# Two chained mixtures of experts after a recurrent attention: the first mixture's second product in float32 for all of F instead of half of it

## The chip, the cores and the metric

The kernel runs on one core of one Trainium2 chip. The metric is the device time of one execution in microseconds (us); the kernel before takes 814.17 us, the median of three runs from 814.04 to 814.33.

## The reference, cut to what matters

```python
# x: (3072, 384), the output of the attention, token by token
def _moe_ref(x, w_gate, w1, w2):               # first mixture, E = 8, F = 1024
    order = np.argsort(-(x @ w_gate).flatten())    # greedy, each expert takes 3072 / 8 = 384 tokens
    ...
    for e in range(E):
        mask = assigned == e
        h = np.maximum(x[mask] @ w1[e], 0.0)       # first product, 384 -> 1024
        out[mask] = h @ w2[e]                      # second product, 1024 -> 384
def _moe2_ref(x, modality_id, w_gate, modality_bias, w1, w2):   # second mixture: the same products,
    ...                                            # each token goes to its best expert and is scaled
```

## The kernel before, in words

The program has three stages on one core. The attention fills the first 235 us or so. Then come the eight experts of the first mixture, one after the other (`job` for j = 0 to 7), until about 560 us, and behind them the second mixture in units of up to 256 tokens (j = 8 and up).

For one expert TensorE (PE) works on 384 gathered tokens. F is cut into eight blocks f of 128. The first product of a block (line 837) has nine matmuls of 384 columns: each float32 operand is split into a high part of type float32r (`w1h`, `xh`) and the remainder (`w1l`, `xl`), and three products high x high, high x low and low x high are added up over three blocks of the 384 inputs. ScalarE (ACT) writes relu of the result to `hh` (line 841).

The second product adds up over f into three PSUM tiles `po`, one for each 128 tokens t. It has two forms, chosen by the table WHOLE for each half of F (blocks 0 to 3 and 4 to 7). In a whole half, `hh` is plain float32, the weights go by DMA straight into the tile `w2h`, and each (f, t) is a single float32 matmul (line 710), which the profile shows as two records of LDWEIGHTS and MATMUL. In a split half the weights land in `wraw`, ACT casts them to a high part (line 753), VectorE (DVE) or, once in the program, GpSimd (POOL) subtracts to get the low part (line 757), DVE makes the remainder `hl` of the hidden values (line 845), and each (f, t) has three matmuls (lines 712, 713, 714). In the kernel before, the experts of the first mixture have their first half whole and their second half split. In the split case the names of the weight pieces both read `w2l` in the profile, since both parts lie in one tile of that name.

While one expert is computed, the same engines prepare the next: `search` finds the next expert's threshold (three passes: DVE compares in `g` line 997, PE counts on line 1010, DVE makes `ind` line 1011, PE sums on line 1024 and, at the end, 1049 from `bm`), `listing` makes the list of its tokens (lines 1096 to 1146) and gathers them to `xg`, and `score2` and `route2` score the finished tokens for the second mixture. All of this is written into the instruction streams by `tick`, a planner that advances coroutines between blocks; each engine then runs its stream strictly in that order and waits by semaphores. Second products are held back in `pend` and flushed in pairs of blocks (blocks 0 and 1, 2 and 3, 4 and 5), 6 and 7 one by one beside the next expert's first blocks.

Of the kernel before, what the change touches and what calls it, by code (L numbers as in the profile page):

```python
# [37 lines left out]
E = 8  # L38
# [393 lines left out]
HALF = (7, 11)  # L432
PICKS = {5: (0, 2, True), 6: (2, 3, True), 7: (3, NU, False)}
NLC = 40
WHOLE = {**{j: 1 for j in range(E)}, E: 2, E + 1: 2, E + 2: 1}
PAGE = 256
GROUPS = {1: 6, 3: 6, 4: 3, 5: 3, 6: 3, 7: 3}
GM = 6
# [147 lines left out]
class Moe:  # L586
# [108 lines left out]
    def w2half(self, j, c):  # L695

        W, n, s = self.W[j], WHOLE.get(j, 0), slice(1536 * c, 1536 * c + 1536)
        if c < n:
# [17 lines left out]
    def weights(self, j, idx, first, every):  # L716
# [4 lines left out]
        def fetch():  # L721
            for h in range(4):
                yield from self.wait(f"lo{j - 1}.{2 * h + 1}")
                if j == 0 and h > 0:
                    yield from self.wait("g0")
                whole = h % 2 and h // 2 < WHOLE.get(j, 0)
                if whole:
# [14 lines left out]
        def split():  # L742
            for q in range(8):
                if q // 2 % 2 and q // 4 < WHOLE.get(j, 0):
                    continue
                yield from self.wait(f"raw{j}.{q // 2}")
                if j == 0 and q == 1:
                    yield from self.wait("x0")
                new = ("w1h", "w1l") if q == 0 else ("w2h", "w2l") if q == 2 else ("w2hl",) if q == 6 and WHOLE.get(j) else ()
                for n in new:  # L750
# [54 lines left out]
    def job(self, j, nt, after):  # L805
# [10 lines left out]
        def second(f, hh, hl, ts=range(nt)):  # L816
            self.until(f"lo{j}.{2 + 4 * (f // 4) + f % 4 // 2}")
            if f == 0:
                st["po"] = [self.po.tile([128, 512], FT, name="po") for _ in range(nt)]
            for t in ts:  # L820
                s = slice(128 * t, 128 * t + 128)
                o = st["po"][t][:, 0:DM]
                self.second_terms(j, f, s, o, hh, hl)
                if f == FB - 1:
                    after(st["po"], t)
            if f == FB - 1 and t == nt - 1:
                del self.W[j]

        for f in range(FB):
# [5 lines left out]
            for k in range(KB):  # L835
                for a, b in ((w1h, xh), (w1h, xl), (w1l, xh)):
                    nc.tensor.matmul(ph, a[:, f // 4, k, s], b[:, k], start=(n == 0), stop=(n == 3 * KB - 1))  # L837
                    n += 1
            whole = f // 4 < WHOLE.get(j, 0)
            hh = self.hp.tile([128, 512], FT if whole else FR, name="hh", bufs=4)[:, 0:T]  # L840
# [8 lines left out]
            self.pend.append(lambda *a, f=f, hh=hh, hl=hl: second(f, hh, hl, *a))  # L849
            keep = PACE["fl"] + (WHOLE.get(j, 0) > 0 and f % 2 == 0 and f > 1)  # L850
            self.flush(keep if f or len(self.pend) < 5 else 3)
# [796 lines left out]
```

## Time and profile before

| quantity | value |
|---|---|
| median of three runs | 814.17 us |
| the profiled execution | 810.52 us |
| its span, first to last instruction | 808.8 us |
| PE busy over the span | 713.9 us, 88% |
| DVE busy over the span | 631.8 us, 78% |
| ACT busy over the span | 352.1 us, 44% |
| POOL busy over the span | 413.1 us, 51% |
| mean granted clock of PE | 0.953 |

The profiled execution is 3.65 us below the median, and its span 1.7 us below its own time. Busy times are unions of the records of an engine, and the records of matmuls that follow each other overlap, because matmuls are pipelined: how long a run of them holds PE is read from the start of the first to the start of what follows.

### The profile page before, as it was taken

To read this page: it belongs to the slowest core of one execution; us is meant where nothing else is said; L and a number is where in the kernel's file an instruction comes from. 1 tells how busy PE (TensorE), PEld (TensorE's weight loads), DVE (VectorE), ACT (ScalarE), POOL (GpSimd) and SP (SyncE) were. 2 spreads that over 40 slices of the span, in tenths; PEclk is the share of its full clock that TensorE was granted. 3 is DMA by queue.
4 is the path that set the end of the run, shared out by engine and by line. 5 is a ranking of instruction groups with operands and counts; after the bars stand their busy time and mean duration, and the time that the engine had idled before them with its cause. 6 is when DMAs were issued, how large, how long until landed. Compare 5 with 4: busy or idle time off the path is not lost.

```text
span 808.8 us, 13793 instructions
## 1 busy us (share of the span) xinstructions
PE 713.9 (88%) x4889; PEld 633.7 (78%) x4889; DVE 631.8 (78%) x1575; ACT 352.1 (44%) x756; POOL 413.1 (51%) x371
## 2 busy tenths in 40 slices
PE   6887778878787798999999999999999999999993
PEld 4776667777754577878787878878778999999993
DVE  7999999999978877687876866847776668677770
ACT  3454545545422224333332433323345556666650
POOL 5788876878715413121211212135558766776640
PEclk8898988889899999999999999999999999999998
DMA  8567767667305235251533424264438766776740
GB/s 284 137 177 174 192 163 183 172 173 193 89 31 186 88 99 173 74 183 50 170 104 112 143 74 157 59 206 138 152 126 288 243 224 218 254 255 219 237 161 24
DMA packets 35199, 129.08 MB, mean 160 GB/s; under 512 B 5225, under 2 KB 14580, under 8 KB 35120
## 3 DMA queue, kind: packets, MB, share of 16 engines
q0 software_dynamic: 17568, 83.82, 30.8%
q1 hardware_dynamic: 16832, 43.95, 20.0%
q8 instruction: 40, 0.66, 0.4%
q10 hardware_dynamic: 720, 0.34, 0.2%
q14 instruction: 39, 0.32, 0.1%
HBM read 113.88 MB, written 14.60 MB: 159 GB/s over the span
## 4 chain that ended last, share of the span: by engine, by line
PE 48%; DVE 30%; issue 10%; DMA 5%; POOL 3%; ACT 2%; POOLq 0%; SPq 0%; DVEq 0%; ACTq 0%
PE ph L837 18%; PE po L710 9%; DVE pf L110 5%; PE po L712 4%; PE po L714 4%; PE po L713 4%; DVE suf L104 3%; DMA ch<-in_ch 2%; DVE pe L116 2%; DMA wraw<-in_w1b,wi 2%; DVE pc L107 2%; PE px L1190 2%; DVE rp L112 2%; DVE g L997 2%; PE px L1010 1%
## 5 line engine op out<-in xcount | busy, mean ns | idle before, releaser
L841 ACT ACTIVATE hh<-ph 128x256 fp32r<-128x256 f32 (+3 forms) x160 | 68.4, 428 | 223.4 <-PE ph L837 204.4
L837 PE MATMUL ph<-xh,w1h 128*128 128x256 f32 (+1 forms) x480 | 154.4, 322 | 1.0 <-DVE hl L845 1.0
L837 PE MATMUL ph<-xl,w1h 128*128 128x256 f32 (+1 forms) x480 | 146.2, 305 | 0.5 <-DVE xl L785 0.2
L837 PE MATMUL ph<-xh,w1l 128*128 128x256 f32 (+1 forms) x480 | 146.3, 305 | 0.0
L139 PE MATMUL pa<-rbd,kh 128*128 128x256 f32 x192 | 64.8, 496 | 46.2 <-ACT rbd L125 46.2
L837 PEld LDWEIGHTS ph<-xh,w1h 128*128 128x128 f32 x480 | 90.6, 189 | 10.6 <-issue 5.0
L837 PEld LDWEIGHTS ph<-xl,w1h 128*128 128x128 f32 x480 | 90.8, 189 | 3.1 <-DVE xl L785 1.4
L710 PE MATMUL po<-w2h,hh 128*128 128x384 f32 x272 | 93.1, 489 | 0.0
L837 PEld LDWEIGHTS ph<-xh,w1l 128*128 128x128 f32 x480 | 90.8, 189 | 0.0
L845 DVE SCALAR_TENSOR_TENSOR hl<-ph,hh 128x256 fp32r<-128x256 f32 (+1 forms) x108 | 49.7, 461 | 51.2 <-ACT hh L841 46.7
L139 PEld LDWEIGHTS pa<-rbd,kh 128*128 128x128 f32 x192 | 45.3, 248 | 56.5 <-POOL ru L131 43.0
L713 PE MATMUL po<-w2l,hh 128*128 128x384 f32 x264 | 88.5, 335 | 0.0
L753 ACT CAST w1h<-wraw 128x768 fp32r<-128x768 f32 x88 | 73.2, 833 | 12.5 <-DMA wraw<-in_w1a,ix 8.8
L498 POOL DMA_INDIRECT wraw<-in_w1a,ix x16 | 16.5, 1034 | 121.3 <-issue 53.0
L710 PEld LDWEIGHTS po<-w2h,hh 128*128 128x128 f32 x272 | 49.5, 190 | 28.8
L757 DVE TENSOR_TENSOR w1l<-wraw,w1h 128x768 fp32r<-128x768 f32 x66 | 64.6, 979 | 7.6 <-ACT w1h L753 7.4
L498 POOL DMA_INDIRECT xg<-xd,ix x24 | 31.3, 1305 | 76.2 <-DVE ix L1146 61.1
L757 POOL TENSOR_TENSOR w1l<-wraw,w1h 128x768 fp32r<-128x768 f32 x22 | 41.2, 1876 | 49.5 <-ACT w1h L753 49.4
L169 ACT ACTIVATE cv<-tk,cb 128x56 f32<-128x56 f32 x192 | 47.2, 328 | 39.2 <-DVE cb L166 39.2
L757 DVE TENSOR_TENSOR w2l<-wraw,w2h 128x768 fp32r<-128x768 f32 x44 | 47.8, 1086 | 11.5 <-ACT w2h L753 11.5
L712 PE MATMUL po<-w2h,hh 128*128 128x384 f32 x160 | 55.2, 345 | 0.0
L714 PE MATMUL po<-w2h,hl 128*128 128x384 f32 x160 | 53.8, 337 | 0.1
(350 smaller groups left out, 1766.9 us busy)
## 6 DMA issues: line engine op xcount, KB each, us to landing
tk<-in_tk SPq DMA_DIRECT2D x24, 608.0 KB, 6.6
ch<-in_ch SPq DMA_DIRECT2D x42, 288.9 KB, 5.4
xd<-y SPq DMA_DIRECT2D x24, 193.0 KB, 2.7
x2d<-x SPq DMA_DIRECT2D x8, 579.0 KB, 4.1
ch<-in_ch SPq DMA_DIRECT2D x23, 192.0 KB, 5.8
ch<-in_ch SPq DMA_DIRECT2D x1, 962.5 KB, 8.8
ch<-in_ch SPq DMA_DIRECT2D x1, 770.5 KB, 8.9
ch<-in_ch SPq DMA_DIRECT2D x2, 256.0 KB, 5.1
```

Source lines behind the costliest of these rows:

```text
L139: nc.tensor.matmul(pa[:, 2 * a:2 * a + 2], t["kh"][:, a], t["rb"][:, a], start=True, stop=True)
L169: nc.scalar.mul(cv[:, h], t["v"][:, DE * h:DE * h + DE], cb[:, h:h + 1])
L498: nc.gpsimd.indirect_dma_start(out=out, out_offset=None, in_=src, in_offset=bass.IndirectOffsetOnAxis(ap=idx, axis=0), bounds_check=bound, ...
L710: mm(o, hh[:, s], w[0][:, hs], start=a, stop=z)
L712: mm(o, hh[:, s], w[0][:, hs], start=a, stop=False)
L713: mm(o, hh[:, s], w[1][:, hs], start=False, stop=False)
L714: mm(o, hl[:, s], w[0][:, hs], start=False, stop=z)
L753: nc.scalar.copy(hi, r)
L757: self.turn[j][q].tensor_tensor(lo, r, hi.bitcast(FT), OP.subtract)
L837: nc.tensor.matmul(ph, a[:, f // 4, k, s], b[:, k], start=(n == 0), stop=(n == 3 * KB - 1))
L841: nc.scalar.activation(hh, ph, AF.Relu)
L845: nc.vector.scalar_tensor_tensor(hl, ph, 0.0, hh.bitcast(FT), op0=OP.max, op1=OP.subtract)
```

## The change

One number of the table WHOLE, which says how many halves of F are whole for expert j.

```diff
@@ -432,7 +432,7 @@
 HALF = (7, 11)
 PICKS = {5: (0, 2, True), 6: (2, 3, True), 7: (3, NU, False)}
 NLC = 40
-WHOLE = {**{j: 1 for j in range(E)}, E: 2, E + 1: 2, E + 2: 1}
+WHOLE = {**{j: 2 for j in range(E)}, E: 2, E + 1: 2, E + 2: 1}
 PAGE = 256
 GROUPS = {1: 6, 3: 6, 4: 3, 5: 3, 6: 3, 7: 3}
```

The table is read in `weights` (whether a half is fetched straight to `w2h` and not split), in `w2half` and `second_terms` (which matmuls), and in `job` (the type of `hh`, whether `hl` is made, and `keep`, whose condition is that WHOLE is over zero and so gives the same numbers as before). On PE the place of every other instruction stays the same; where the three split matmuls of an (f, t) stood, one float32 matmul stands. So on PE, in the first expert's block 6 (the tiles `po` are the three token blocks), before:

```order
L1049 MATMUL px_3091<-bm_87,ones_415 128x16
L712 MATMUL po_2766<-w2l_2681,hh_2938 128x384
L713 MATMUL po_2766<-w2l_2681,hh_2938 128x384
L714 MATMUL po_2766<-w2l_2681,hl_2940 128x384
L712 MATMUL po_2767<-w2l_2681,hh_2938 128x384
L713 MATMUL po_2767<-w2l_2681,hh_2938 128x384
L714 MATMUL po_2767<-w2l_2681,hl_2940 128x384
L712 MATMUL po_2768<-w2l_2681,hh_2938 128x384
L713 MATMUL po_2768<-w2l_2681,hh_2938 128x384
L714 MATMUL po_2768<-w2l_2681,hl_2940 128x384
L837 MATMUL ph_3125<-xh_2942,w1h_2905 128x384
```

and now, at the same place on PE:

```order
L1049 MATMUL px_3064<-bm_87,ones_415 128x16
L710 MATMUL po_2760<-w2h_2503,hh_2927 128x384
L710 MATMUL po_2761<-w2h_2503,hh_2927 128x384
L710 MATMUL po_2762<-w2h_2503,hh_2927 128x384
L837 MATMUL ph_3092<-xh_2929,w1h_2894 128x384
```

Nine rows became three, and what stands ahead and behind is the same.

On DVE, in the third expert, between the routing for the second mixture (lines 1225, 1227) and the search's `ind`, before:

```order
L1225 TENSOR_REDUCE mxo<-eq_3832 128x6
L845 SCALAR_TENSOR_TENSOR hl<-ph,hh 128x384
L1201 TENSOR_REDUCE se<-ex 128x3
L1202 TENSOR_SCALAR se<-se 128x3
L1203 RECIPROCAL x_3643<-se 128x3
L1204 COPY x_3643<-xg 128x3
L1011 TENSOR_SCALAR ind<-px,rem 8x64
```

and now, at the same place on DVE:

```order
L1225 TENSOR_REDUCE mxo<-eq_3749 128x6
L1201 TENSOR_REDUCE se<-ex 128x3
L1202 TENSOR_SCALAR se<-se 128x3
L1203 RECIPROCAL x_3561<-se 128x3
L1204 COPY x_3561<-xg 128x3
L1011 TENSOR_SCALAR ind<-px,rem 8x64
```

Only `hl` is gone from ahead of `ind`; the subtractions of line 757 for `w2l` go from DVE in the same way.

On POOL, in the first expert, the gathers of weights and the one subtraction that POOL has for the second product, before:

```order
L498 DMA wraw<-in_w1a,ix 128x1536
L498 DMA wraw<-in_w2a,ix 128x1536
L757 TENSOR_TENSOR w1l<-wraw,w1h 128x3x256 x2
L757 TENSOR_TENSOR w2l<-wraw,w2l 128x768
L498 DMA wraw<-in_w1a,ix 128x1536
```

and now, at the same place on POOL:

```order
L498 DMA wraw<-in_w1a,ix 128x1536
L498 DMA w2h<-in_w2a,ix 128x1536
L757 TENSOR_TENSOR w1l<-wraw,w1h 128x3x256 x2
L498 DMA wraw<-in_w1a,ix 128x1536
```

The gather of the second half has the same size and place and another target, and the subtraction is gone.

## Rows read from the trace of the kernel before

**Rows 1.** Windows: stretch, length, busy us (instructions), PE clock, DMA share, GB/s.

```profile
348.36:386.00 37.64, 35.37 (x274) 30.49 (x274) 30.05 (x115) 12.95 (x25) 8.96 (x7) 1.00 0.30 98
...
560.00:600.00 40.00, 40.00 (x238) 31.75 (x239) 29.80 (x106) 15.14 (x32) 18.81 (x15) 1.00 0.53 184
```

**Rows 2.** Waits of PE, 255 to 560 us: waiter, releaser, us, times, longest.

```profile
PE px L1010 <- DVE g L997: 7.0, 5, 2.2
PE px L1024 <- DVE ind L1011: 5.8, 7, 1.2
...
PE px L1049 <- DVE bm L1039: 1.8, 4, 0.7
PE px L1242 <- DVE tb L1234: 1.8, 2, 1.3
...
PE px L1111 <- DVE ef L1102: 1.3, 1, 1.3
PE px L1326 <- DVE vv L1320: 0.5, 1, 0.5
PE ph L837 <- DVE hl L845: 0.3, 1, 0.3
```

**Rows 3.** Timeline of PE in one expert: start, us, line, shapes, idle before.

```profile
350.94 4.12 PE L710 MATMUL po<-w2h,hh 128*128 128x384 f32 x12
354.89 0.73 PE L1190 MATMUL px<-wg,xt 128*128 128x8 f32 x6
...
362.10 4.04 PE L710 MATMUL po<-w2h,hh 128*128 128x384 f32 x12
365.97 0.49 PE L778 MATMUL px<-ident,xg 128*128 128x128 f32 x3
...
371.55 0.42 PE L712 MATMUL po<-w2l,hh 128*128 128x384 f32 x1
...
374.76 0.33 PE L837 MATMUL ph<-xh,w1h 128*128 128x384 f32 x1
...
376.32 0.33 PE L712 MATMUL po<-w2l,hh 128*128 128x384 f32 x1
...
377.88 0.33 PE L837 MATMUL ph<-xh,w1h 128*128 128x384 f32 x1
```

**Rows 4.** Instructions on tile `po`: duration ns min/median/max, starts, forms.

```profile
L710 PE MATMUL po<-w2h,hh x272: 483/486/590, 272.1 to 610.7; 128*128 128x384 f32 x136
...
L713 PE MATMUL po<-w2l,hh x264: 331/334/346, 295.5 to 795.5; 128*128 128x384 f32 x132
```

**Rows 5.** Timeline of DVE and PE around 360 us.

```profile
358.69 0.55 DVE L845 SCALAR_TENSOR_TENSOR hl<-ph,hh 128x384 fp32r<-128x384 f32 x1
...
359.75 0.26 DVE L1011 TENSOR_SCALAR ind<-px,rem 8x64 bf16<-8x64 f32 x1
...
360.07 0.19 PE L1024 MATMUL px<-ind,ones 128*128 128x64 bf16 x1 [1.19 <-DVE ind L1011]
```

**Rows 6.** Timeline of POOL, DVE and PE in the first expert.

```profile
265.93 1.87 POOL L757 TENSOR_TENSOR w2l<-wraw,w2l 128x768 fp32r<-128x768 f32 x1 [0.63 <-ACT w2l L753]
...
266.37 1.46 DVE L1163 COPY md<-xg 128x3 f32<-128x3 f32 x1
...
300.80 0.15 DVE L1163 COPY md<-xg 128x3 f32<-128x3 f32 x1
...
269.01 0.94 DVE L757 TENSOR_TENSOR w2l<-wraw,w2l 128x768 fp32r<-128x768 f32 x1
...
268.86 0.17 PE L1049 MATMUL px<-bm,ones 128*128 128x16 bf16 x1 [0.66 <-DVE bm L1039]
...
272.02 0.16 PE L1111 MATMUL px<-inc,tri 128*128 128x1 bf16 x1 [1.30 <-DVE ef L1102]
```

**Rows 7.** Timeline of POOL: two gathers of one expert.

```profile
380.65 1.00 POOL L498 DMA_INDIRECT w2h<-in_w2a,ix  x1 [0.30 <-PE po L714]
...
395.05 1.59 POOL L498 DMA_INDIRECT xg<-xd,ix  x1 [9.42 <-DVE ix L1146]
```

## The prediction, made before the changed kernel ran

> **What bounds the kernel now.** I read the windows by stage first. In a steady expert of the first mixture PE is busy 35.37 of 37.64 us at a granted clock of 1.00 (the upper of its two levels, 2.4 GHz), DVE 30.05, ACT 12.95; in the second mixture PE is busy all 40.00 us of a window [rows 1]. So from the second expert on PE sets the pace, with some 2.3 us an expert (37.64 - 35.37) in which it waits. Next I read for whom: between 255 and 560 us the waits of PE that DVE ended add up to 7.0 + 5.8 + 1.8 + 1.8 + 1.3 + 0.5 + 0.3 = 18.5 us [rows 2], nearly all of them links of the search for the next expert, a chain that goes from PE to DVE and back. Two things thus count in this change: what it does to PE's own work, and how much of those 18.5 us hangs on the DVE, ACT and POOL work that it takes away. Last I read PE's timeline, from the start of a run of matmuls to the start of what follows it, since the records overlap.
>
> **PE's own work.** For each expert the second half has 4 blocks x 3 token blocks = 12 (f, t), 96 in the 8 experts. In a split half PE goes through blocks 4 and 5 (18 matmuls) from 371.55 to 374.76, in 3.21 us, and through block 6 (9 matmuls) from 376.32 to 377.88, in 1.56 us, 0.173 us a matmul and so 0.52 us an (f, t) [rows 3]. Block 7 has the same nine, so 1.56 again; the three runs make 3.21 + 2 x 1.56 = 6.33 us an expert. In a whole half a pair of blocks (6 float32 matmuls, 12 records) takes 350.94 to 354.89, 3.95 us, where it stands behind a small bf16 matmul, and 362.10 to 365.97, 3.87 us, where it does not [rows 3]: 0.645 us an (f, t), two records of 0.32. In the changed kernel the pair 4, 5 stands behind the bf16 matmul of line 1049, so 3.95; blocks 6 and 7 are half a pair each, together 3.87. That is 7.82 us. The float32 form thus costs PE 7.82 - 6.33 = 1.49 us more an expert, and 8 x 1.49 = 11.9 us in all. It all lies on the engine that sets the pace, so this is the main term, and it makes the kernel slower.
>
> The Trainium skill has a rule on this (FP8 and Floating Point Precision, TensorE Precision Notes): true FP32 makes four passes through the array, while FP32 at reduced precision is read and truncated. The trace agrees in its direction, 0.645 us against 0.52 [rows 3]; it does not agree in the size that counting passes would give, which is a rival below.
>
> **What goes from the other engines.** Each expert loses four `hl` on DVE, 0.55 us each [rows 5], two subtractions of `w2l`, 0.94 us on DVE [rows 6], one of the 16 on POOL, 1.87 us [rows 6], and two casts on ACT. PE gains only where such an instruction stands ahead of a link that PE waits for. I went through PE's waits one by one:
>
> - Experts 2 to 4, `ind` behind `hl`: DVE runs without a pause from the token scores to `ind` at 359.75, with `hl` at 358.69 in between, and PE waits 1.19 us for it [rows 5]. Without `hl` the `ind` comes one slot of about 0.5 us earlier (its 0.55 us overlap their neighbours a little). 3 x 0.5 = 1.5 us, with what the wait for `bm` may gain.
> - The first expert is bound by the search. POOL's subtraction runs 265.93 to 267.80, and during it a copy of three elements a partition, `md`, takes 1.46 us on DVE where the same copy later takes 0.15 [rows 6]. With the subtraction gone DVE is 1.3 us earlier at `bm`, and PE's wait of 0.66 us ahead of line 1049 goes; PE also starts that matmul some 0.15 us earlier because the queue ahead of it is empty: 0.8 us. Then DVE's own `w2l` subtraction at 269.01 stands between `bm` and the list, and PE waits 1.30 us for the list at 272.02 [rows 6]; I let 1.1 of it go. Two `hl` further on stand ahead of a `g` and an `ind`: 0.3 and 0.4. Together 2.6 us.
> - The last expert: the routing chain that ends in `vv` is held up by an `hl` that waits for ACT; the waits of 0.5 for `vv` and 0.3 for an `hl` go [rows 2]: 0.8 us.
> - Others stay. The long waits for `g` in the second expert and for `tb` in experts 6 and 7 (1.3 the longest) [rows 2] end chains in which no removed instruction stands.
>
> The sum of the relief is 1.5 + 2.6 + 0.8 = 4.9, with 0.3 for small ones 5.2 us. Its bounds are 0, if another link is late in place of each, and 18.5 us, all that DVE ended [rows 2]. I take 5.2, since each term has its own row or place, and most of the 18.5 is the round trip itself.
>
> **What moves.** The second half's weights now land in the whole tile `w2h`, two of which exist. The gather for expert j + 1 must wait until expert j - 1 has finished with all eight blocks, where four were enough. In POOL's queue that gather stands at 380.65, when PE is at the last products of block 7 of that very expert [rows 7]. With the longer float32 products it would start perhaps 2 us later. Behind it stand two more gathers and then the gather of tokens, ahead of which POOL is idle for 9.42 us [rows 7]; the weights of those gathers are wanted an expert later. So I cost it at nothing; without that cover it would be 2 us an expert. The number of bytes stays, and on ACT nothing that PE waits for stood behind the two casts but in the first expert, which is counted above.
>
> **The sum.** 11.9 - 5.2 = 6.7 us. Made against the profiled execution: 810.52 + 6.7 = 817.2. The median of the runs shown is 3.65 us above that execution, and I carry the difference along: 814.17 + 6.7 = 820.9 us. No term lies behind 560 us, where PE is full and its instructions are the same, so the delay reaches the end.
>
> **The rivals.**
>
> 1. The relief does not come: each wait that goes is taken over by the next link of the same chain, which is a round trip and not a queue. Then only PE's work counts, 814.17 + 11.9 = 826.1. For it speaks that DVE often stands idle for PE in the chain; against it that in rows 5 and 6 DVE works without a pause ahead of the link.
> 2. The relief is much greater, and the kernel gets faster. The mechanism is the search chain on DVE: with 4 us less DVE work an expert the chain runs ahead, and all PE's waits on it vanish. The end of this is 11.9 - 18.5 = -6.6, 807.6 us; it decides for faster from the point where more than 11.9 + 1.6 of the 18.5 us go. For it speaks DVE's load of 30.05 us in 37.64 [rows 1]; against it that `g`, the largest entry, is waited for where no removed instruction precedes it. I would put this case at about 811.
> 3. The duration of a record is its price. The float32 record takes 486 ns and the split one 334 [rows 4], so an (f, t) would take 2 x 486 = 972 ns against 3 x 334 = 1002, and 96 x 0.03 = 2.9 us would be won on PE, before any relief: 814.17 - 2.9 - 5.2 = 806.1. Against it stands rows 3, where the same records start 0.32 and 0.17 us apart. The Trainium skill has the reason to choose by the starts (Trainium Kernel Development and Optimization, Performance Expectations): matmul busy time is a bad metric because matmuls are pipelined.
> 4. A float32 matmul costs four times a split one, 4 x 0.173 = 0.69 us, and the rows of a float32 pair understate it, because the run behind it starts late. Then 96 x (0.69 - 0.52) = 16.3, less 5.2, gives 814.17 + 11.1 = 825.3. This is what the rule on four passes named above would make of the row of the split form. Against it stands the pair's own rows, 3.87 us for six [rows 3].
>
> **How the numbers follow.** Forecast 0.75, rival 1 0.10, rival 2 0.06, rival 3 0.03, rival 4 0.06. Around the forecast the relief can be some 3 us more or less, 817.5 to 824. The range takes in most of rivals 1 and 4 above and a part of rival 2 below: 816 to 825.5. A measurement of this kernel can tell a change of 0.2%, 1.6 us, from none. Slower than 815.8 are the forecast, rivals 1 and 4 and a small part of the rest: 0.91. Within 812.5 to 815.8 lies part of rival 2, 0.04; faster the rest of 2 and rival 3, 0.05.
>
> **What would show it.** In the profile after: line 710 has 464 records and not 272, 0.32 us apart in the second half too; no line 757 or 753 on `w2l` before 560 us and 32 fewer `hl`; a steady expert is 38.6 us long and not 37.64, of which PE's busy part has grown by 1.5; the wait for `ind` in experts 2 to 4 is 0.7 and not 1.2; `md` in the first expert takes 0.15 us and the first pair of second products starts some 2 us earlier. The prediction is wrong if the steady expert keeps its length or gets shorter, if line 710 starts closer together than now, or if a new wait of PE for `w2h` appears.

## The result, and the profile after

In the first comparison the changed kernel took 823.18 us (median of four, 820.97 to 824.98) and the kernel before, run beside it, 814.25 (four, 814.04 to 814.99): a ratio of 1.0107, 95% interval 1.008 to 1.0133, or +8.7 us. It is slower, as forecast; the forecast's 820.9 us is a ratio of 1.0082. Two later comparisons with more runs, on other occasions, gave 1.006 (1.0033 to 1.0086) and 1.0053 (1.0025 to 1.008), +4.9 and +4.3 us. The forecast lies inside the first two intervals and just above the third; the mean of the three is +6.0 us. What the runs show of why they differ stands in the next section.

The windows of the profile after, one expert and a stretch of the second mixture, at the places of [rows 1]:

```profile
354.97:393.02 38.05, 36.69 (x262) 28.63 (x261) 26.93 (x109) 11.54 (x23) 8.42 (x8) 1.00 0.34 113
572.00:612.00 40.00, 40.00 (x238) 31.75 (x239) 27.77 (x98) 15.10 (x32) 18.74 (x15) 1.00 0.51 176
```

The expert is 38.05 us long where it was 37.64. PE's busy time grew by 1.32, DVE's fell by 3.12 and ACT's by 1.41; the expert grew by only 0.41, so some 0.9 us of waits went. It was forecast to become 38.6 us long with 1.5 more of PE's work: the direction held, the growth was less than half. The waits of PE from 255 to 560 us, beside [rows 2]:

```profile
PE px L1010 <- DVE g L997: 7.8, 6, 2.2
...
PE px L1024 <- DVE ind L1011: 3.0, 6, 0.7
PE px L778 <- DMA xg<-xd,ix: 1.8, 3, 0.9
PE px L778 <- DVE ec L1332: 1.8, 1, 1.8
PE px L1242 <- DVE tb L1234: 1.8, 2, 1.3
```

`ind` went from 5.8 us to 3.0, and the waits for `bm` (1.8), `ef` (1.3), `vv` (0.5) and `hl` (0.3) are gone. `g` and `tb` stay. Two entries look new and are not. The wait for `ec` is that of a matmul which waited before as well, for `xg`:

```profile
473.28 0.52 PE L778 MATMUL px<-ident,xg 128*128 128x128 f32 x3 [1.62 <-DMA xg<-xd,ix]
```

```profile
482.07 0.52 PE L778 MATMUL px<-ident,xg 128*128 128x128 f32 x3 [1.83 <-DVE ec L1332]
```

(the first is before, the second after; a second profile of the kernel before names a third releaser there, `R`, with 1.69). And of the 1.8 us for `xg` after, 1.3 are waits at the start of the first expert, which lie ahead of 255 us in the kernel before; the other 0.50, at 406.48, is new. PE in the expert of [rows 3], from block 4 on:

```profile
377.12 0.18 PE L1049 MATMUL px<-bm,ones 128*128 128x16 bf16 x1
377.16 4.12 PE L710 MATMUL po<-w2h,hh 128*128 128x384 f32 x12
380.82 0.64 PE L837 MATMUL ph<-xh,w1h 128*128 128x384 f32 x1
381.30 0.33 PE L837 MATMUL ph<-xl,w1h 128*128 128x384 f32 x1
...
382.68 2.10 PE L710 MATMUL po<-w2h,hh 128*128 128x384 f32 x6
384.32 0.63 PE L837 MATMUL ph<-xh,w1h 128*128 128x384 f32 x1
384.79 0.34 PE L837 MATMUL ph<-xl,w1h 128*128 128x384 f32 x1
```

The first matmul behind a float32 run is followed by the next one after 0.48 and 0.47 us instead of 0.17, so the run's price is read to that second start, less 0.17 (to the first start it would be 3.66 and 1.64, too little, since the rest of it stands in the successor): 381.30 - 377.16 - 0.17 = 3.97 us for the pair and 384.79 - 382.68 - 0.17 = 1.94 for one block. The three runs make 3.97 + 2 x 1.94 = 7.85, where 7.82 was forecast. The tile `po` in the view of durations, as in [rows 4]:

```profile
L710 PE MATMUL po<-w2h,hh x464: 482/486/1000, 275.7 to 623.5; 128*128 128x384 f32 x155
```

It has the 464 records foretold, at the same 486 ns; the longest, 1000 ns, belongs to a stretch at the low clock. Of `hl` (line 845) there are 76 where 108 were, 32 fewer as foretold. DVE and PE at the place of [rows 5]:

```profile
365.30 0.17 DVE L1201 TENSOR_REDUCE se<-ex 128x3 f32<-128x24 f32 x1
...
365.85 0.26 DVE L1011 TENSOR_SCALAR ind<-px,rem 8x64 bf16<-8x64 f32 x1
...
366.16 0.19 PE L1024 MATMUL px<-ind,ones 128*128 128x64 bf16 x1 [0.68 <-DVE ind L1011]
```

No `hl` stands there, and the wait is 0.68 instead of 1.19. The first expert, beside [rows 6]:

```profile
271.24 0.15 DVE L1163 COPY md<-xg 128x3 f32<-128x3 f32 x1
...
273.67 0.18 PE L1049 MATMUL px<-bm,ones 128*128 128x16 bf16 x1
...
275.67 0.16 PE L1111 MATMUL px<-inc,tri 128*128 128x1 bf16 x1
```

`md` takes 0.15 us, and neither matmul has a wait for DVE ahead of it any more. For the waits this is not yet proof, because they depend on where PE's clock is low: the first expert is unchanged in `c_rest` and `d_none567` (below), and there too the wait for `bm` is absent and that for `ef` is 0.80 and 0.65, with the low stretch at 268 to 274 us, while in the kernel before it lies at 261 to 265 (read in windows of 1 us). The profile `e_first`, with the changed first expert and the low stretch at 260 to 264, is the one to set beside it:

```profile
268.27 0.18 PE L1049 MATMUL px<-bm,ones 128*128 128x16 bf16 x1
...
270.26 0.16 PE L1111 MATMUL px<-inc,tri 128*128 128x1 bf16 x1
```

Neither waits. The gathers, beside [rows 7]:

```profile
388.71 1.02 POOL L498 DMA_INDIRECT w2h<-in_w2a,ix  x1 [5.48 <-PE po L710]
...
402.14 1.60 POOL L498 DMA_INDIRECT xg<-xd,ix  x1 [8.11 <-DVE ix L1146]
```

The gather of weights now does wait for PE, and starts 8.06 us later than before; PE itself is 6.75 later there, so the wait costs it 1.3 (one expert earlier 3.0, one later 2.5). The gather of tokens is 7.09 later and POOL is still idle ahead of it: the delay is covered, and PE waits nowhere for `w2h`.

### The profile page after: what moved, and what is told of

Read it like the earlier page. It is cut to its first block, busy times and chain, and to the rows that moved or that the text cites. A ratio compares the mean times of both kernels' runs of the same rounds, so it can differ in the third digit from the quotient of the medians.

```text
span 821.9 us, 13510 instructions
## 1 busy us (share of the span) xinstructions
PE 732.3 (89%) x4793; PEld 626.1 (76%) x4793; DVE 600.5 (73%) x1528; ACT 340.4 (41%) x740; POOL 411.9 (50%) x370
## 4 chain that ended last, share of the span: by engine, by line
PE 50%; DVE 8%; issue 7%; DMA 2%; POOL 2%; ACT 1%; POOLq 0%; ACTq 0%; DVEq 0%
PE ph L837 18%; PE po L710 15%; PE po L712 3%; PE po L714 3%; PE po L713 3%; PE px L1190 2%; PE px L778 2%; PE px L1010 1%; DMA wraw<-in_w1b,wi 1%; DVE g L997 1%; PE ph L894 1%; DVE w1l L757 1%; DMA xg<-xd,ix 1%; PE px L1185 1%; POOL out L1502 1%
## 5 line engine op out<-in xcount | busy, mean ns | idle before, releaser
L841 ACT ACTIVATE hh<-ph 128x256 fp32r<-128x256 f32 (+2 forms) x160 | 68.3, 427 | 240.5 <-PE ph L837 204.9
L837 PE MATMUL ph<-xh,w1h 128*128 128x256 f32 (+1 forms) x480 | 160.5, 334 | 1.9 <-DVE hl L845 1.2
L710 PE MATMUL po<-w2h,hh 128*128 128x384 f32 x464 | 161.5, 494 | 0.0
L710 PEld LDWEIGHTS po<-w2h,hh 128*128 128x128 f32 x464 | 85.7, 192 | 48.8 <-issue 1.5
L139 PE MATMUL pa<-rbd,kh 128*128 128x256 f32 x192 | 67.0, 510 | 42.8 <-ACT rbd L125 42.8
L498 POOL DMA_INDIRECT wraw<-in_w1a,ix x16 | 20.0, 1253 | 114.0 <-issue 72.0
L757 DVE TENSOR_TENSOR w1l<-wraw,w1h 128x768 fp32r<-128x768 f32 x66 | 62.9, 954 | 7.7 <-ACT w1h L753 7.2
L845 DVE SCALAR_TENSOR_TENSOR hl<-ph,hh 128x256 fp32r<-128x256 f32 x76 | 32.0, 422 | 34.9 <-ACT hh L841 28.0
L713 PE MATMUL po<-w2l,hh 128*128 128x384 f32 x168 | 56.4, 336 | 0.0
L712 PE MATMUL po<-w2h,hh 128*128 128x384 f32 x160 | 55.1, 344 | 0.0
```

What stands on the lines that cost most here:

```text
L139: nc.tensor.matmul(pa[:, 2 * a:2 * a + 2], t["kh"][:, a], t["rb"][:, a], start=True, stop=True)
L498: nc.gpsimd.indirect_dma_start(out=out, out_offset=None, in_=src, in_offset=bass.IndirectOffsetOnAxis(ap=idx, axis=0), bounds_check=bound, ...
L710: mm(o, hh[:, s], w[0][:, hs], start=a, stop=z)
L712: mm(o, hh[:, s], w[0][:, hs], start=a, stop=False)
L713: mm(o, hh[:, s], w[1][:, hs], start=False, stop=False)
L757: self.turn[j][q].tensor_tensor(lo, r, hi.bitcast(FT), OP.subtract)
```

## Where the difference lies, and how much of it is chance

I cut the span at three rows of PE that every kernel has: the first matmul of line 1049, the one of line 1111 in the first expert's last blocks, and the last of line 1242 ahead of the second mixture. In the kernel before:

```profile
241.47 0.17 PE L1049 MATMUL px<-bm,ones 128*128 128x16 bf16 x1
...
305.32 0.18 PE L1111 MATMUL px<-inc,tri 128*128 128x1 bf16 x1
...
571.56 0.17 PE L1242 MATMUL px<-tb,ones 128*128 128x8 bf16 x1
```

and in the second profile of the changed kernel (`c_after` below):

```profile
244.42 0.17 PE L1049 MATMUL px<-bm,ones 128*128 128x16 bf16 x1
...
307.94 0.17 PE L1111 MATMUL px<-inc,tri 128*128 128x1 bf16 x1
...
580.48 0.17 PE L1242 MATMUL px<-tb,ones 128*128 128x8 bf16 x1
```

The stretches between such rows, worked out for every profile (us; the experts counted from j = 0, cut at further rows of line 1111; the clock is that of 255 to 300 us):

```
kernel       attention  j=0 (clock)   j=1    j=2-4   j=5-7   behind
before         241.47   63.85 (.96)  36.56  112.98  116.70   237.2
c_before       241.03   63.88 (.96)  36.60  112.90  116.81   236.9
e_before       243.98   65.66 (.89)  36.58  112.94  116.96   240.4
after          244.87   66.09 (.89)  37.18  114.96  120.43   238.4
c_after        244.42   63.52 (.96)  37.19  114.98  120.37   237.7
e_after        243.02   65.85 (.89)  37.18  115.16  120.44   237.8
c_first        243.83   65.27 (.92)  36.63  112.82  116.78   237.0
e_first        240.71   63.14 (.96)  36.59  112.83  117.38   238.4
c_rest         244.11   65.57 (.92)  37.18  115.15  120.49   237.1
d_price        240.93   65.49 (.96)  37.14  117.28  120.81   238.1
d_relief       244.55   63.90 (.92)  36.16  112.08  115.53     -
d_none567      245.00   65.57 (.92)  36.56  113.16  123.19   237.3
d_none17       243.04   64.10 (.96)  36.05  116.83  120.17   237.2
```

From j = 1 to 7 kernels with the same code repeat to 0.6 us or better. The attention and the first expert don't: they move by some 3 and 2 to 3 us between profiles of the same kernel, with the granted clock. Two windows (218 to 235 and 255 to 300 us) in the kernel before, first profile, and in its third, `e_before`:

```profile
218.00:235.00 17.00, 14.16 (x123) 11.66 (x122) 13.63 (x39) 6.31 (x20) 6.79 (x8) 1.00 0.10 36
255.00:300.00 45.00, 35.38 (x286) 28.49 (x285) 34.44 (x100) 11.99 (x21) 15.45 (x11) 0.96 0.39 133
```

```profile
218.00:235.00 17.00, 13.89 (x98) 12.13 (x97) 11.38 (x32) 6.39 (x20) 5.46 (x8) 0.80 0.07 24
255.00:300.00 45.00, 35.31 (x293) 28.24 (x294) 32.57 (x89) 12.56 (x22) 16.60 (x13) 0.89 0.42 141
```

The same program is at the lower level (0.5, 1.2 GHz) for longer in these two places, and ends its attention 2.5 us and its first expert another 1.8 us later. Its times ran from 809 to 819 us over the three occasions. Not all of that is the clock: `e_before` is also 3.2 us longer behind 571 us, at the same 0.98 clock there; PE has two waits of 1.0 us in it that the first profile lacks, for `xg` and for ACT's `x`, and the rest was not located.

Equal mean clock is not enough for the first expert either; the low stretch has to lie in the same place. Three pairs have that: `e_first` against before (260 us) is 0.7 us shorter, `c_first` against `c_rest` (268 and 285) 0.3 shorter, `e_after` against `e_before` (264 to 276) 0.2 longer. `c_after` (269 to 273 alone) has no such partner.

## The experiments

**The kernel before and after again, and the change in two parts.** `c_before` and `c_after` have no edit; the parts differ from the changed kernel in the table alone (the names behind # are added here).

```diff
-WHOLE = {**{j: 2 for j in range(E)}, E: 2, E + 1: 2, E + 2: 1}
+WHOLE = {0: 2, **{j: 1 for j in range(1, E)}, E: 2, E + 1: 2, E + 2: 1}     # c_first
+WHOLE = {0: 1, **{j: 2 for j in range(1, E)}, E: 2, E + 1: 2, E + 2: 1}     # c_rest
```

Expected of `c_before`: 

> The kernel before once more, for a second profile of it on another occasion. Theory (the low-clock stretches of PE in the attention and in the first expert differ from one execution to the next by chance): the first expert's dip to the 0.5 clock may be longer or shorter than the 3.4 us of the first profile, at the same or another place, and the time lies within 810 to 815 us. Rival (the dips belong to the program): one dip of 3.4 us at the same place again.

Expected of `c_after`: 

> The changed kernel once more, timed in five rounds. Theory of the prediction (price 11.9 us, relief 5.2): +6.7 us. What the first result left open: it gave +8.9 us, and its profile has 6.8 + 3.4 us at the 0.5 clock in the first expert where before had 3.4. If the dips are chance, the timed difference is between +6 and +9 and this profile shows another dip pattern; if the change causes them, the profile shows the two dips again and the difference stays at +8.5 to +9.5.

Expected of `c_first`: 

> Only the first expert has the float32 form in both halves, the other seven are as before. Theory (price 1.49, relief 2.6 in the first expert): -1.1 us. Rival 1 (no relief): +1.5 us. A third reading, that the clock dips of the first expert come with this part of the change: about +1.8 us.

Expected of `c_rest`: 

> Experts 1 to 7 have the float32 form in both halves, the first expert is as before. Theory (7 x 1.49 = 10.4, relief 1.5 + 0.8 + 0.3 = 2.6): +7.8 us. Rival 1 (no relief): +10.4 us. If the sum of both parts holds, this and the run with only the first expert add up to the whole change (+8.9 as timed so far).

Measured: `c_before` 809.96 us; against a kernel before of 811.1 (median of 23) `c_after` 1.006 (1.0033 to 1.0086), `c_first` 0.9964 (0.9943 to 0.9985), `c_rest` 1.0099 (1.0064 to 1.0134), so +4.9, -2.9 and +8.0 us; the parts add up to 5.1. By the rows, `c_first` changes j = 0 only and `c_rest` all but that, as built. The second profile of the changed kernel has the 0.96 clock in the first expert that before had, and there the expert is 0.33 us shorter, not 2.2 longer as in the first profile: the further low-clock stretches don't come with the change (`e_before` below has them without it).

**Price without relief.** In `d_price` PE does the changed products, while casts, subtractions and `hl` are still made and nobody reads them (cut to the conditions; the casts now read the tile `w2h`, for which PE waits nowhere in this run either).

```diff
+                dummy = j < E and q in (6, 7)
-                if q // 2 % 2 and q // 4 < WHOLE.get(j, 0):
+                if q // 2 % 2 and q // 4 < WHOLE.get(j, 0) and not dummy:
...
-            if not whole:
+            if not whole or (j < E and f >= 4):
```

Expected: 

> The changed products on PE, but the work that the change takes from DVE, ACT and POOL is done all the same: the casts and subtractions of w2l go from the whole tile into a tile that nobody reads, and hl is made for blocks 4 to 7 and not used. Theory (price 11.9, and the relief of 5.2 hangs on exactly this work): +11.9 us against the kernel before, some 5 more than the changed kernel, 10.5 to 13 with the spread of the runs. Rival (the relief does not hang on it, and the price on PE is smaller than forecast): the same as the changed kernel, +6 to +9.

Measured: 821.87 against 811.0 us, 1.0127 (1.0094 to 1.016), +10.3. By the rows, with the first profile's clock: +1.64, +0.58, +4.30 and +4.11 in j = 0, 1, 2-4 and 5-7, +10.6 in all. The waits of PE from 255 to 560 us, whose lines stand eight higher in this kernel:

```profile
PE px L1018 <- DVE g L1005: 7.3, 5, 2.3
PE px L1032 <- DVE ind L1019: 5.8, 7, 1.2
...
PE px L1057 <- DVE bm L1047: 2.1, 4, 0.9
...
PE px L1119 <- DVE ef L1110: 1.3, 1, 1.3
```

`ind`, `bm` and `ef` are waited for as in [rows 2], and the low stretch lies at 260 to 265 us as it did there: those waits hung on the removed work.

**Relief without price.** In `d_relief` PE keeps three split matmuls, with other operands, and the work is gone; half of the second product is left out of the output. A further line, not shown, keeps `hh` of these blocks in the split form's type.

```diff
+        if j < E and f >= 4:
+            w, hl = (self.W[j]["w1h"][:, 1536:3072], self.W[j]["w1l"][:, 1536:3072]), hh
```

Expected: 

> The other half of the change: PE keeps three split matmuls for each (f, t) of blocks 4 to 7, but the casts and subtractions of w2l and the hl of those blocks are not made. The three matmuls take the first product's weight tiles and hh as stand-in operands, so half of the second product of the first mixture is left out of the output. Theory: -5.2 us against the kernel before. Rival 1 (each wait that goes is replaced by the next link of the round trip): 0. Rival 2 (the chain runs ahead): -10 or more. Price and relief measured apart should add up to what the whole change gives, +6 to +9.

Measured: 866.77 us, which says nothing, because the second mixture routes its tokens by the first one's output, and its work changes with it. Up to 571 us the rows hold. The first expert is 1.67 us shorter than in the two kernels that have the old first expert with low stretches at the same places (`c_rest`, `d_none567`); j = 1, 2-4 and 5-7 are 0.40, 0.90 and 1.17 shorter than before: 4.1 us in all. Price and relief apart make 10.6 - 4.1 = 6.5; the change itself makes 6.0 by the same stretches (`c_after` against before). That the sums come so close is partly luck: for j = 2-4 the parts give 4.30 - 0.90 = 3.4 where the change has 2.0, and for j = 5-7 4.11 - 1.17 = 2.9 where it has 3.7. Where price and relief act on the same waits they can't be added.

**The change turned round.** If a float32 (f, t) costs more than a split one, taking the other half's float32 away should win.

```diff
+WHOLE = {**{j: 0 if j in (5,6,7) else 1 for j in range(E)}, ...}            # d_none567
+WHOLE = {**{j: 0 if j in (1,2,3,4,5,6,7) else 1 for j in range(E)}, ...}    # d_none17
...
-            keep = PACE["fl"] + (WHOLE.get(j, 0) > 0 and f % 2 == 0 and f > 1)
+            keep = PACE["fl"] + ((WHOLE.get(j, 0) > 0 or j < E) and f % 2 == 0 and f > 1)
```

The second pair of lines, in both, keeps the order in which second products are flushed as it is in the kernel before.

Expected of `d_none567`: 

> The change turned round for experts 5, 6 and 7: split products in both halves, the other five experts as before. Theory (the price of 1.49 an expert works both ways, and the routing that these experts wait for holds none of the added work): 3 x -1.49 = -4.5 us. Rival (the added hl and w2l subtractions stand ahead of what PE waits for there): up to 0.5 to 1 us an expert given back, -2 to -3; if DVE becomes the bound, 0 or slower.

Expected of `d_none17`: 

> The change turned round for experts 1 to 7: split products in both halves, the first expert as before. PE's work falls by 7 x 1.49 = 10.4 us, DVE's grows by 4 x 0.55 + 2 x 0.94 = 4.1 us an expert, from 30.05 to 34.1 us in an expert of then 36.2. Theory (the relief's mirror image: every added hl or subtraction ahead of a link costs its slot, about as much as the change won, 2.6 to 5 us): -5 to -8 us. Rival (DVE becomes the bound): 0 or slower. Rival 1 read backwards (no relief, so nothing to lose either): -10.4.

Measured: 1.0097 (1.0063 to 1.0131) and 1.0101 (1.0057 to 1.0145), both about 8 us slower. My theory was wrong, and so was rival 1 read backwards; the sign is that of the rival put at 0 or slower. The third expert in the kernel before and in `d_none17`, and what PE waits for in the latter:

```profile
341.88:379.44 37.56, 35.29 (x273) 30.42 (x273) 29.32 (x111) 12.95 (x25) 6.17 (x7) 1.00 0.33 115
```

```profile
343.19:381.47 38.28, 33.78 (x285) 32.11 (x285) 32.80 (x118) 14.39 (x27) 6.90 (x7) 1.00 0.33 114
```

```profile
PE px L1190 <- ACT xt L1187: 2.1, 1, 2.1
PE px L1024 <- DVE ind L1011: 2.0, 1, 2.0
```

In the kernel before these waits are 0.7 and 1.2 (`xt` and `ind`). PE lost 1.5 us of work, and the two waits behind ACT and DVE grew by 2.2. In other experts the clock fell as well. The sixth to eighth expert of `d_none567` in three windows, and the middle one's counterpart in the kernel before:

```profile
460.29:497.59 37.30, 34.10 (x217) 33.18 (x216) 27.14 (x106) 14.30 (x27) 8.57 (x8) 0.91 0.33 117
497.59:549.53 51.94, 47.14 (x297) 45.26 (x296) 37.53 (x146) 19.47 (x39) 14.37 (x13) 0.93 0.34 111
549.53:583.48 33.95, 31.09 (x195) 28.05 (x196) 23.99 (x94) 12.75 (x27) 14.44 (x11) 1.00 0.57 203
```

```profile
489.58:538.42 48.84, 45.89 (x278) 39.52 (x278) 30.12 (x131) 17.84 (x36) 12.98 (x12) 1.00 0.42 137
```

The clock is 0.91 and 0.93 where before had 1.00 throughout. At the lower level are 0.09 x 37.30 / 0.5 + 0.07 x 51.94 / 0.5 = 14.0 us, worth up to half of that, 7.0 (split matmuls start 0.32 us apart there and not 0.17), and the stretch grew by 6.5. `d_none17` has 0.96, 0.96 and 0.93 in the fourth, fifth and seventh window of an expert (39.92, 38.63 and 51.97 us), worth up to 6.8, and its seven experts grew by 6.8 together. So with the most that the clock can have cost taken off, these experts are about as long as before, though by the price of 1.49 PE has 4.5 and 10.4 us less to do: about that much the chains behind DVE and ACT took back, as seen for the third expert and by the sum for the others. PE waited for `xt` shortly ahead of the first fall:

```profile
465.57 0.83 PE L1190 MATMUL px<-wg,xt 128*128 128x8 f32 x6 [1.48 <-ACT xt L1187]
...
467.43 0.33 PE L837 MATMUL ph<-xl,w1h 128*128 128x384 f32 x1
...
468.12 0.53 PE L837 MATMUL ph<-xl,w1h 128*128 128x384 f32 x1
```

That the wait brings the fall was not tried: the kernel before and the changed one have a wait of 1.6 and 1.8 ahead of line 778 in the sixth expert and no fall. There is one profile of each of these kernels, so how regularly they meet the low clock is open.

**A third round.** No edit but that of `c_first`.

Expected of `e_before`: 

> The kernel before, a third profile. Theory (how many 3.4 us stretches at the 0.5 clock fall on PE before 300 us is chance, and with them a time of 809 to 815): a profile of 809 to 811 us has the pattern of the first two, one of 813 to 815 us has a further stretch near 221 or 286 us. Rival (the pattern belongs to the kernel): 6.8 us near 210, none near 221, 3.4 us near 261, whatever the time.

Expected of `e_after`: 

> The changed kernel, a third timing, since the first two gave +8.9 and +6.0. By the rows of its second profile (first gating instruction to the first unit of the second mixture: +6.0, and +0.5 behind it): +6 to +6.5 us. If the further stretches at the low clock come with the change: +8.5 to +9.5.

Expected of `e_first`: 

> The first expert alone in float32, a second timing. By the rows (price 1.49, of the relief 1.8): -0.3 us, no difference that can be measured. By its first timing: -2.5 us. If the timing again lies under -1.2, the rows miss something that this kernel wins.

Measured: `e_before` 818.21 us, with the longer low-clock stretches shown above, so these are no mark of the change, and `e_first` (profiled at 810.74 us) has the pattern of the first profile of the kernel before, with the change in its first expert. `e_after` 1.0053 (1.0025 to 1.008) and `e_first` 1.0001 (0.9979 to 1.0023). The -2.9 us of `c_first` did not come back; I don't call the first expert alone an improvement, and no kernel tried beats the one before for certain.

## Why the prediction was right, step by step

- **PE's price.** The size of a run was right, 7.85 us against 7.82. What reached the time was 10.6 us, not 11.9 (`d_price`). The claim that "it all lies on the engine that sets the pace" failed there: part of the longer runs fell into waits of PE that stood until then. To find them the stretches have to be counted right. Block 7 of the first expert stands ahead of the row of line 1111 at 305.32 that cuts the stretches, block 7 of the later ones behind it (the first row below is of the first expert, the others of the second, before):

```profile
303.75 0.33 PE L712 MATMUL po<-w2l,hh 128*128 128x384 f32 x1
...
341.88 0.18 PE L1111 MATMUL px<-inc,tri 128*128 128x1 bf16 x1
341.94 0.43 PE L712 MATMUL po<-w2l,hh 128*128 128x384 f32 x1
```

  So j = 1 holds three quarters of a price, 1.12, and j = 5-7 three and a quarter, 4.84; measured are 0.58 and 4.11. In j = 0 (1.64 for 1.49) and j = 2-4 (4.30 for 4.47) nearly all of it arrived. In j = 1 the longer run covers the wait for `xl` in the second expert, which `d_price` doesn't have:

```profile
337.25 0.45 PE L837 MATMUL ph<-xl,w1h 128*128 128x384 f32 x1 [0.20 <-DVE xl L785]
```

  From line 1049 to block 6 the kernel before takes 2.15 us there (336.60 to 338.75), `d_price` 1.68 (338.38 to 340.06): 0.47 of the 0.54. In j = 5-7 it covers the waits for `vv` and `hl` of the last expert, 0.47 and 0.28, which is the 0.73. These two places make 1.2 of the 1.3 us that were forecast too much.
- **Experts 2 to 4.** Forecast 1.5, measured 4.30 - 2.00 = 2.3 (`d_price` against `c_after`). The slot of `ind` was right, 1.19 to 0.68. Too small was "with what the wait for `bm` may gain": that wait went in all three as well, and from the start of the matmul ahead to line 1049 it is 0.18 us now (373.96 to 374.14, `c_after`) where it was 0.73 (370.78 to 371.51), so 3 x 0.5 + 3 x 0.55 = 3.2. Of this 0.7 went to the next link, a wait for `xg` that was not there before (403.48 in `c_after`). That is rival 1's mechanism, for a part. Taken alone (`d_relief`) the relief was 0.9 there. Its waits of PE in these three experts, 344.6 to 456.7 us, have `ind` at 1.7 where before had 3.5, and no `bm`, where before had 1.2; but `xg`, which was not waited for, takes 2.2 of those 3.0 us back; as I read it, PE without the longer products is still further ahead of the gathers:

```profile
PE px L780 <- DMA xg<-xd,ix: 2.2, 2, 1.5
...
PE px L1026 <- DVE ind L1013: 1.7, 3, 0.7
```

- **The first expert.** Forecast 2.6, measured 2.4 (`d_price` against `e_first`, low stretch at the same place), 2.0 (against `c_after`) and 1.7 (`d_relief`). The mechanism held: `md` takes 0.15 us in all six profiles without POOL's subtraction of `w2l`, and 0.70 to 1.70 in the seven with it, where it always ends with the subtraction (at 267.83 and 267.80 us in the first profile, 271.54 and 271.52 in `e_before`, where it starts late in it). It held term by term in `e_first` against before: from the matmul ahead to line 1049 0.18 us (268.09 to 268.27) where it was 1.00 (267.86 to 268.86), 0.82 for 0.8; from there to line 1111 1.99 where it was 3.16, 1.17 for 1.1; the `g` at 280.32 is waited for 1.85 and not 2.21, 0.36 for 0.3; the `ind` behind it no longer, 0.40 for 0.4. (That the stretch shows less than their sum goes with a wait of 0.72 for ACT's `xh` at 255.58, which `d_price` doesn't have.) Wrong was that the first pair of second products starts 2 us earlier: counted from the first row of line 1049 it is 29.6 us against 30.6. The stretch's net, forecast -1.1, is -0.7, -0.3 and +0.2 in the three pairs.
- **The last experts.** Forecast 0.8 + 0.3, measured 4.11 - 3.67 = 0.4. The waits for `vv` and `hl` did go, but they are gone in `d_price` too, where the work was kept: PE comes later and no longer meets them. I counted them as relief; they are cover of the price.
- **What moves.** The gather starts 1.3 to 3.0 us later against PE (2 forecast) and costs nothing, as forecast.
- **The sum.** By rows, -0.3 + 0.6 + 2.0 + 3.7 = 6.0 up to 571 us, for a forecast of 6.7: a price 1.3 too high and a relief 0.6 too high, which partly cancel; so far the sum is better than its terms by luck. With the pairs' -0.7 to +0.2 for the first expert it is 5.6 to 6.5. Behind 571 us the three profiles after (237.7 to 238.4) lie inside those of before (236.9 to 240.4).
- **The rivals.** Rival 1 (no relief, +11.9) falls by `d_price`: with the relief taken away the kernel is slower still, 10.6 against 6.0 by the rows, though its mechanism took the 0.7 us for `xg`. Rival 2 (all waits go) falls by `g` and `tb`, which stayed. Rivals 3 and 4 fall by the 7.85 us of a half, since rival 3 would have it under the split form's 6.33 and rival 4 at 12 x 0.69 = 8.3.

What the forecast took as settled, that 814.17 us against 810.52 is a constant to carry along, is not so: the same program moves by 3.0 us in the attention and 1.8 in the first expert, with its low-clock pattern, and by 3.5 behind 571 us. No run near 814 us was profiled in that comparison, so which of these made up the 3.65 us is not shown. Nor can a measurement tell 0.2% here: the first comparison, of four runs, is 2.7 us above the 6.0 of the rows, and `c_first` moved from -2.9 to +0.1.

## What to carry to other kernels

Price a change on the pacing engine from start to start, read past the first matmul behind the run, and then take off what the longer runs push into waits that already stand: a wait can be ended by making its waiter late, which is not relief. Before a wait is called new or gone, find its instruction in the other trace: the releaser's name can change while the wait stays, and a wait can go because the clock was low elsewhere. A small gain that comes with taking work off a second engine does not turn round: when the same trade was driven the other way, the chains behind the other engines took back about all that PE saved, and low clock came on top. And when executions of one kernel differ by more than the effect, compare the stretches between common rows, with the low clock at the same place, rather than totals.

## What the runs showed that I had not expected

The granted clock fell to 0.91 and 0.93 in windows of steady experts of `d_none567`, where the kernel before, with more float32 matmuls in the same places, had 1.00; `d_none17` had 0.96, 0.96 and 0.93 in three such windows. So in these two profiles a kernel with less work on PE got the lower clock; why is open. And the attention has at least two clock patterns in one and the same program, 241.0 and 244.0 us to its end, of which `e_before` and `c_before` each show one.
